# Attention's probability transposes in 64-row halves on two row tiles, and the last 64 keys' product in two 64-column tiles

## The chip, the cores and the metric

One core of a Trainium2 chip runs the program once. The metric is device time in microseconds (us) of one execution. A run's profile names the core's engines: PE is TensorE's matmul side and PEld its weight loads, DVE is VectorE, ACT is ScalarE, POOL is GpSimd, SP is SyncE.

## The reference

Attention with a learned relative-position bias, and two mixture layers behind it, all in float32:

```python
scores = scale * np.matmul(q, k.transpose(0, 1, 3, 2))
...
bias = h @ w2
scores = scores + bias.transpose(2, 0, 1)[None, :, :, :]
scores = scores - np.max(scores, axis=-1, keepdims=True)
attn = np.exp(scores)
attn = attn / (np.sum(attn, axis=-1, keepdims=True) + 1e-09)
return np.matmul(attn, v).astype(np.float32)
```

There are 4 batches, 8 heads, 576 positions and 64 values a head. The change touches the attention alone.

## The kernel before, in words

**Units, chunks and steps.** A unit is four heads of one batch (`UNITS`, 8 of them). The 576 query rows are cut into a chunk of 64 and four of 128 (`CH`); R is the rows of a chunk. A step works on one chunk, one unit and one pair of heads, so there are 80 of them. The first group of steps (`GROUPS[0]`, three units, 30 steps) also computes the bias table of each chunk as it goes; later groups have one unit each and read the finished table.

**What a step does.** `qk` (L313) makes the scores of both heads: the two heads lie on partitions 0 to 63 and 64 to 127, so their matmuls go to two row tiles (`tile_position=(64 * i, 0)`) and to separate PSUM buffers `sc`. VectorE then adds the bias and takes the row minimum of the negated scores (L328). ScalarE exponentiates and sums (L336); VectorE inverts the sums (L342, L343); GpSimd scales the rows (L345). `pv_tr` (L350) turns the probabilities, R rows of 2 x 576 keys, into nine blocks of 128 keys by R rows: eight blocks of one head each, and a ninth that holds the last 64 keys of both heads. It does three blocks per call: three transposes on TensorE into one PSUM bank (L358), and one copy into the SBUF buffer `eT`, by ScalarE (L361) or VectorE (L363) as the strings `EVAC0` and `EVAC` say. `pv` (L365) multiplies V with these blocks: the eight blocks in two column tiles, one per head (L373), and the ninth block with a 128-column matrix `vt` that has each head's last 64 keys in its own rows and columns and zeros elsewhere (L375). ScalarE copies the result out (L378), and one DMA per two steps writes it to HBM (L380).

A float32 matmul leaves two records in the trace and a transpose one, so a step has 8 records at L325, 9 at L358, 16 at L373 and 2 at L375.

**Order.** The steps are pipelined by hand. In one pass of the loop in `emit` (L382) step s has its scores, step s-1 its exponentials and sums, step s-3 its transposes and step s-4 its product with V. The strings `ORDER0` (first group) and `ORDER` (later groups) give the order in which the pass issues them: Q0 and Q1 are the two heads' scores and reductions, X0 and X1 the exponentials, T0 to T2 the three calls of `pv_tr`, P the product, N the normalisation, S other loads and preparations, B a piece of the bias. Each engine takes its instructions in that order. S also holds the conversion of the next layer's weights, on ScalarE and VectorE.

**PSUM.** The scores use four banks. The four others (`banks`, L139) rotate: each call of `mix` (L145) takes the next, whoever used it last. A later taker waits for the earlier one's copy.

Of the kernel before, what the change touches and what calls it, by code (L numbers as in the profile page):

```python
# [15 lines left out]
B, H, S, D = 4, 8, 576, 64  # L16
P = 128
# [7 lines left out]
GROUPS = [[0, 1, 2], [3], [4], [5], [6], [7]]  # L25
# [4 lines left out]

ORDER0 = "Q0 T0 X0 B Q1 X1 B S T1 B P B B B N T2"
ORDER = "T0 S T1 X0 X1 Q0 Q1 P N T2"

OUT = {"A": "AAA", "D": "AVV", "T": "VAA"}

EVAC0 = "VAAVAV"
EVAC = "VAVAAV"

# [90 lines left out]
def flat(t):  # L133
    return t.rearrange("p a b -> p (a b)")
# [24 lines left out]
class Attn(Base):  # L159
# [74 lines left out]
    def bias_mm(self, c, blk, ts):  # L234
        nc = self.nc
        r0, R = CH[c]
        ncg = 4 // (R // 64)
        kind = KIND[c][blk]
        pb = self.mix([4 * R], "pb")
        for cg in range(4):  # L240
            nc.tensor.matmul(pb[32 * cg:32 * cg + 32, :], self.w2b[:, 0, :], flat(ts[cg // ncg][:, cg % ncg]),
                             start=True, stop=True, tile_position=(0, 32 * cg))
        i = self.bti = getattr(self, "bti", -1) + 1
        bt = self.tl(f"bt{i % 2}", [4, R])
        pv = pb.rearrange("p (a r) -> p a r", a=4)
        if kind == "A":
            (nc.scalar.copy if OUT["A"][0] == "A" else nc.vector.tensor_copy)(bt, pv)
        elif kind == "D":
            if OUT["D"][0] == "A":
                nc.scalar.activation(bt, pv, AF.Identity, bias=self.cb)  # L250
            else:
                nc.vector.tensor_scalar(bt, pv, self.cb, None, op0=ALU.add)
        else:
            nc.vector.scalar_tensor_tensor(bt, self.lib[c][0][:, 0:1, :].to_broadcast([P, 4, R]), self.cb, pv, op0=ALU.mult, op1=ALU.add)
        return bt
# [94 lines left out]
    def pv_tr(self, c, u, pr, es, eT, gi):  # L350
        nc = self.nc
        r0, R = CH[c]
        e, st = es
        ef = flat(e[:R])
        src = [ef[:, j * 640 + kb * 128:j * 640 + (kb + 1) * 128] for kb in range(4) for j in range(2)] + [ef[:, 512:640]]
        pt = self.mix([3, 128], "pt")
        for i in range(3):
            nc.tensor.transpose(pt[:, i, :R], src[3 * gi + i], self.ident[:R, :R])  # L358
        d = eT[:, 3 * gi:3 * gi + 3, :]
        if (EVAC0 if u in GROUPS[0] else EVAC)[3 * pr + gi] == "A":  # L360
            nc.scalar.copy(d, pt[:, :, :R])  # L361
        else:
            nc.vector.tensor_copy(d, pt[:, :, :R])  # L363

    def pv(self, s, c, u, pr, eT):  # L365
        nc = self.nc
        b, hf = UNITS[u]
        r0, R = CH[c]
        vm, vt = self.v[u]
        po = self.mix([R], "po")  # L370
        for kb in range(4):
            for j in range(2):
                nc.tensor.matmul(po[64 * j:64 * j + 64, :], vm[:, 2 * pr + j, kb, :], eT[:, 2 * kb + j, :],  # L373
                                 start=kb == 0, stop=False, tile_position=(0, 64 * j), skip_group_check=True)
        nc.tensor.matmul(po, vt[:, pr, :], eT[:, 8, :], start=False, stop=True, skip_group_check=True)  # L375
        if pr == 0:
            self.xo = self.tl(f"xo{s // 2 % 2}", [2, R])
        nc.scalar.copy(self.xo[:, pr, :], po)  # L378
        if pr == 1:
            nc.sync.dma_start(self.xT_d[2 * hf:2 * hf + 2, :, b * S + r0:b * S + r0 + R].rearrange("q p r -> p q r"), self.xo)  # L380

    def emit(self, extra):  # L382
# [89 lines left out]
        for s in range(N + 4):  # L472
# [16 lines left out]
            if a:  # L489
                es[s] = self.new_e(s)  # L490
            for k in (ORDER0 if g0 else ORDER).split():
                if k[0] == "Q" and a:
# [888 lines left out]
```

## Time and profile before

| | |
|---|---|
| median of 3 runs | 1086.18 us (1084.26 to 1088.27) |
| the profiled execution | 1088.37 us, span 1086.6 us |
| TensorE | 1044.1 us busy, 96% of the span |
| VectorE | 617.9 us busy, 57% |
| ScalarE | 538.7 us busy, 50% |
| GpSimd | 220.7 us busy, 20% |

A row of a timeline gives start and length in us, then engine, line, operation, the tile written and the tile read, the partitions and columns, how many instructions the row merges, and in brackets how long the engine was idle before and what ended that. A row of groups gives the count, the busy time and the mean length of one. A row of stretches gives, for each engine, its busy time and its number of instructions.

### The profile page before, as it was taken

Reading aid. Unit: us, or ns where it says so; the run is one execution under the profiler, and the core shown is the slowest. Engines: PE = TensorE matmul, PEld = TensorE weight load, DVE = VectorE, ACT = ScalarE, POOL = GpSimd, SP = SyncE. Lnnn points to the kernel's source line nnn. Section 1 sums busy time; section 2 is a strip of 40 time slices with the busy share of each in tenths; the row PEclk is TensorE's granted clock in tenths of the full one; section 3 lists DMA queues with packets and bytes.
Section 4 is the critical chain, followed back from the end, with each engine's and each line's share of the span. In section 5 each row is a group of like instructions: output and inputs, shape, how many; then the busy total and the mean of one; then the engine's idle time right before and its main releaser. Section 6 shows DMA issues by size and latency. Waiting matters only on the chain. (4 is left out here: it accounts for less than half of the span.)

```text
span 1086.6 us, 20980 instructions
## 1 busy us (share of the span) xinstructions
PE 1044.1 (96%) x7637; PEld 814.8 (75%) x7637; DVE 617.9 (57%) x1554; ACT 538.7 (50%) x1198; POOL 220.7 (20%) x273
## 2 busy tenths in 40 slices
PE   5999999999999989999999999999999989999996
PEld 2355556767777778988888889888887868777774
DVE  4886875678776776776354443436364634345320
ACT  4778777667776655544343333333343223354421
POOL 0132223444444300000011000001311242221111
PEclk9999999999999999999999999999999989999998
DMA  7565582333233233431102010110412175676840
GB/s 237 178 191 167 162 274 58 94 96 96 79 83 108 70 110 104 129 117 58 59 21 40 1 40 8 33 39 2 152 64 41 48 254 213 245 289 263 335 165 34
DMA packets 62192, 129.19 MB, mean 119 GB/s; under 512 B 13820, under 2 KB 35708, under 8 KB 59264
## 3 DMA queue, kind: packets, MB, share of 16 engines
q1 hardware_dynamic: 57424, 117.69, 33.1%
q0 software_dynamic: 4512, 9.49, 3.0%
q8 instruction: 62, 1.02, 0.4%
q10 hardware_dynamic: 144, 0.59, 0.2%
q14 instruction: 50, 0.41, 0.2%
HBM read 164.08 MB, written 14.65 MB: 164 GB/s over the span
## 5 line engine op out<-in xcount | busy, mean ns | idle before, releaser
L701 PE MATMUL acc<-wp,g 128*128 128x512 f32 x864 | 225.4, 396 | 0.7 <-DVE t L678 0.6
L671 PE MATMUL ph<-xh,wp 128*128 128x256 f32 x1024 | 207.1, 285 | 1.6 <-ACT y L714 1.2
L345 POOL TENSOR_SCALAR e<-e,st 128x576 f32<-128x576 f32 (+1 forms) x160 | 126.6, 803 | 244.2 <-DVE st L343 190.2
L671 PEld LDWEIGHTS ph<-xh,wp 128*128 128x128 f32 x1024 | 166.4, 189 | 10.9 <-issue 3.9
L701 PEld LDWEIGHTS acc<-wp,g 128*128 128x128 f32 x864 | 153.1, 189 | 27.6 <-DVE t L678 1.2
L328 DVE CUSTOM_DVE_ANT_0 e<-sc,bias 128x576 f32<-128x576 f32 (+1 forms) x160 | 116.4, 751 | 62.4 <-PE sc L325 60.1
L671 PE MATMUL ph<-xl,wp 128*128 128x256 f32 x512 | 144.3, 282 | 0.3 <-DVE xl L657 0.3
L677 ACT ACTIVATE r<-ph,small 128x256 f32<-128x256 f32 x144 | 67.5, 469 | 123.4 <-PE ph L671 118.3
L336 ACT ACTIVATE e<-e,st 128x576 f32<-128x576 f32 (+1 forms) x160 | 123.0, 775 | 0.0
L678 DVE SCALAR_TENSOR_TENSOR t<-r,ph 128x256 f32<-128x256 f32 x144 | 60.3, 419 | 107.4 <-ACT r L677 99.6
L680 ACT ACTIVATE g<-t 128x256 fp32r<-128x256 f32 x144 | 60.2, 418 | 115.0 <-DVE t L678 114.1
L1024 PE MATMUL peh<-ws,xt 128*128 128x512 f32 x408 | 102.7, 405 | 4.5 <-PEq L1333 4.4
L325 PE MATMUL sc<-K,q 64*128 64x288 f32 (+1 forms) x640 | 101.9, 425 | 0.0
L358 PE MATMUL pt<-cst,e 128*128 128x128 f32 (+1 forms) x720 | 97.8, 268 | 2.7 <-ACT eT L361 1.4
L358 PEld LDWEIGHTS pt<-cst,e 128*128 128x128 f32 (+1 forms) x720 | 75.8, 141 | 31.9 <-issue 14.9
L671 PEld LDWEIGHTS ph<-xl,wp 128*128 128x128 f32 x512 | 96.7, 189 | 3.9 <-DVE xl L657 0.5
L775 POOL DMA_INDIRECT tab_d<-small x18 | 18.5, 1029 | 379.5 <-DVE small L773 343.5
L1024 PEld LDWEIGHTS peh<-ws,xt 128*128 128x128 f32 x408 | 76.9, 192 | 22.5 <-issue 5.0
L683 DVE SCALAR_TENSOR_TENSOR g<-t,g 128x256 fp32r<-128x256 f32 x144 | 61.1, 424 | 56.1 <-ACT g L680 55.7
L1052 PE MATMUL peo<-ws,ehh 128*128 128x512 f32 x272 | 86.1, 398 | 0.0
L373 PEld LDWEIGHTS po<-eT,V 128*64 128x64 f32 x1280 | 63.3, 136 | 24.6 <-issue 18.5
L373 PE MATMUL po<-eT,V 128*64 128x128 f32 (+1 forms) x1280 | 81.2, 269 | 0.0
(215 smaller groups left out, 1451.5 us busy)
## 6 DMA issues: line engine op xcount, KB each, us to landing
er<-in_we SPq DMA_DIRECT2D x46, 1024.0 KB
er<-in_we SPq DMA_DIRECT2D x86, 512.0 KB
xb<-in_xb SPq DMA_DIRECT2D x38, 512.0 KB
wraw<-in_wf SPq DMA_DIRECT2D x32, 512.0 KB
cv<-in_xb SPq DMA_DIRECT2D x11, 512.0 KB
K<-in_kT SPq DMA_DIRECT2D x8, 576.0 KB
xr<-xT_d SPq DMA_DIRECT2D x9, 512.0 KB
y_d<-y SPq DMA_DIRECT2D x18, 256.0 KB
```

Source lines behind the costliest of these rows:

```text
L325: nc.tensor.matmul(self.sc[i][:R, n, :288], q[d, pr, :], self.kv[u][d, pr, n * 288:(n + 1) * 288], start=True, stop=True, tile_position=(6 ...
L328: nc.vector.tensor_tensor_reduce(out=e[:R, j, :].rearrange("p (n s) -> p n s", n=2), in0=self.sc[j][:R, :, :288], in1=self.bias[c][:R, 4 * ...
L336: self.nc.scalar.activation(e[:R, j, :], e[:R, j, :], AF.Exp, scale=-1.0, bias=st[:R, j:j + 1], accum_out=st[:R, 4 + j:5 + j])
L345: nc.gpsimd.tensor_scalar(e[:R, j, :], e[:R, j, :], st[:R, 6 + j:7 + j], 1.0, op0=ALU.mult, op1=ALU.mult)
L358: nc.tensor.transpose(pt[:, i, :R], src[3 * gi + i], self.ident[:R, :R])
L373: nc.tensor.matmul(po[64 * j:64 * j + 64, :], vm[:, 2 * pr + j, kb, :], eT[:, 2 * kb + j, :], start=kb == 0, stop=False, tile_position=(0, ...
L671: nc.tensor.matmul(ph, w, x[c], start=n == 0, stop=n == 11)
L677: nc.scalar.activation(r, ph, AF.Relu, bias=self.three)
L683: nc.vector.scalar_tensor_tensor(g[:, 1], t, 1.0 / 6.0, g[:, 0].bitcast(F32), op0=ALU.mult, op1=ALU.subtract)
L701: nc.tensor.matmul(acc[t], x, w, start=f == 0 and i == 0, stop=f == 15 and i == 2)
L1024: nc.tensor.matmul(ph[:, n, :], a, w, start=c == 0 and i == 0, stop=c == 3 and i == 2)
L1052: nc.tensor.matmul(d["po"], a, w, start=f == 0 and i == 0, stop=f == 7 and i == 2)
```

## The change

The nine blocks of a step are transposed in two calls instead of three, the first with five blocks and the second with four. In a chunk of 128 rows each block is transposed as two halves of 64 rows, each half on a row tile of its own and into a PSUM bank of its own; ScalarE copies the lower halves out and VectorE the upper ones. In the chunk of 64 rows there is one half; ScalarE copies the first call's blocks and VectorE the second's. The ninth block's product with `vt` is issued as two matmuls of 64 columns, in the column tiles of the other eight. T2 leaves the orders.

```diff
-ORDER0 = "Q0 T0 X0 B Q1 X1 B S T1 B P B B B N T2"
-ORDER = "T0 S T1 X0 X1 Q0 Q1 P N T2"
+ORDER0 = "Q0 T0 X0 B Q1 X1 B S T1 B P B B B N"
+ORDER = "T0 S T1 X0 X1 Q0 Q1 P N"
...
-EVAC0 = "VAAVAV"
-EVAC = "VAVAAV"
+EVAC = 0
...
-        pt = self.mix([3, 128], "pt")
-        for i in range(3):
-            nc.tensor.transpose(pt[:, i, :R], src[3 * gi + i], self.ident[:R, :R])
-        d = eT[:, 3 * gi:3 * gi + 3, :]
-        if (EVAC0 if u in GROUPS[0] else EVAC)[3 * pr + gi] == "A":
-            nc.scalar.copy(d, pt[:, :, :R])
-        else:
-            nc.vector.tensor_copy(d, pt[:, :, :R])
+
+        a, z = ((0, 5), (5, 9))[gi]
+        hs = range(R // 64)
+        pts = [self.mix([z - a, 64], "pt") for _ in hs]
+        for i in range(a, z):
+            for h in hs:
+                d = slice(64 * h, 64 * h + 64)
+                nc.tensor.transpose(pts[h][:, i - a, :], src[i][d], self.ident[d, d], tile_position=(64 * h, 0))
+        for h in hs:
+            d = eT[:, a:z, 64 * h:64 * h + 64]
+            if (h if R == 128 else gi) == EVAC:
+                nc.scalar.copy(d, pts[h])
+            else:
+                nc.vector.tensor_copy(d, pts[h])
...
-        nc.tensor.matmul(po, vt[:, pr, :], eT[:, 8, :], start=False, stop=True, skip_group_check=True)
+
+        for j in range(2):
+            nc.tensor.matmul(po[64 * j:64 * j + 64, :], vt[:, pr, 64 * j:64 * j + 64], eT[:, 8, :],
+                             start=False, stop=True, tile_position=(0, 64 * j), skip_group_check=True)
```

## Rows read from the trace of the kernel before

**Rows 1.** The page: TensorE's busy time and the clock granted to it.

```profile
PE 1044.1 (96%) x7637; PEld 814.8 (75%) x7637; DVE 617.9 (57%) x1554; ACT 538.7 (50%) x1198; POOL 220.7 (20%) x273
...
PEclk9999999999999999999999999999999989999998
```

**Rows 2.** Groups at L325 on TensorE, from 85.1 to 172.7 and 195.8 to 368.7.

```profile
L325 PE MATMUL sc<-K,q 64*128 64x288 f32 x112 | 17.4, 429 | 0.0
...
L325 PE MATMUL sc<-K,q 64*128 64x288 f32 (+1 forms) x392 | 63.4, 425 | 0.0
```

**Rows 3.** Stretches: length, PE, PEld, DVE, ACT, POOL, clock, DMA share, GB/s.

```profile
85.10:172.70 87.60, 86.22 (x739) 51.58 (x738) 63.40 (x147) 69.57 (x153) 22.97 (x28) 1.00 0.60 191
...
195.80:368.70 172.90, 171.46 (x1717) 128.94 (x1715) 127.91 (x385) 121.16 (x328) 77.61 (x108) 1.00 0.34 94
```

**Rows 4.** Timeline of TensorE's matmuls over one step of 128 rows.

```profile
333.01 0.49 PE L375 MATMUL po<-eT,VT 128*128 128x128 f32 x2
333.34 1.15 PE L358 MATMUL pt<-cst,e 128*128 128x128 f32 x9
334.41 1.24 PE L325 MATMUL sc<-K,q 64*128 64x288 f32 x8
335.58 1.09 PE L373 MATMUL po<-eT,V 128*64 128x128 f32 x16
336.61 0.38 PE L375 MATMUL po<-eT,VT 128*128 128x128 f32 x1
```

**Rows 5.** Timeline of TensorE's weight loads over the same step.

```profile
333.23 1.02 PEld L358 LDWEIGHTS pt<-cst,e 128*128 128x128 f32 x9
334.41 0.79 PEld L325 LDWEIGHTS sc<-K,q 64*128 64x128 f32 x8 [0.17 <-issue]
335.58 0.85 PEld L373 LDWEIGHTS po<-eT,V 128*64 128x64 f32 x16 [0.39 <-issue]
```

**Rows 6.** Timeline of TensorE and its loads, transposes of a 64-row chunk.

```profile
316.01 0.77 PE L358 MATMUL pt<-cst,e 64*128 64x64 f32 x9
316.62 1.82 PE L325 MATMUL sc<-K,q 64*128 64x288 f32 x8
...
316.00 0.63 PEld L358 LDWEIGHTS pt<-cst,e 64*128 64x128 f32 x9
```

**Rows 7.** Timeline of the weight loads that start between 334.40 and 334.45.

```profile
334.41 0.19 PEld L325 LDWEIGHTS sc<-K,q 64*128 64x128 f32 x2 [0.17 <-issue]
```

**Rows 8.** Groups of the copies out of PSUM after transposes, by form.

```profile
L363 DVE COPY eT<-pt 128x384 f32<-128x384 f32 x96 | 51.5, 550 | 3.7 <-PE pt L358 3.6
...
L361 ACT COPY eT<-pt 128x384 f32<-128x384 f32 x96 | 44.7, 482 | 23.7 <-PE pt L358 17.6 <-DVE eT L363 2.9 <-DVE st L342 1.5
...
L363 DVE COPY eT<-pt 128x192 f32<-128x192 f32 x24 | 8.3, 344 | 0.0
L361 ACT COPY eT<-pt 128x192 f32<-128x192 f32 x24 | 7.2, 317 | 3.9 <-DVE eT L363 1.9 <-PE pt L358 1.8 <-ACT xo L378 0.2
```

**Rows 9.** Timeline of VectorE, the reductions of the step of rows 4.

```profile
335.79 0.76 DVE L328 CUSTOM_DVE_ANT_0 e<-sc,bias 128x576 f32<-128x576 f32 x1 [0.91 <-PE sc L325]
...
336.48 0.75 DVE L328 CUSTOM_DVE_ANT_0 e<-sc,bias 128x576 f32<-128x576 f32 x1
```

**Rows 10.** Timeline of ScalarE in that step: output copy and an exponential.

```profile
333.54 0.27 ACT L378 COPY xo<-po 128x128 f32<-128x128 f32 x1 [0.52 <-PE po L375]
...
334.94 0.78 ACT L336 ACTIVATE e<-e,st 128x576 f32<-128x576 f32 x1
```

**Rows 11.** Timeline of TensorE, two score starts of the first group without bias work.

```profile
172.76 1.24 PE L325 MATMUL sc<-K,q 64*128 64x288 f32 x8
...
176.51 0.76 PE L325 MATMUL sc<-K,q 64*128 64x288 f32 x4
```

**Rows 12.** Timeline of TensorE, three transposes in a bias step, then the product.

```profile
112.39 0.49 PE L358 MATMUL pt<-cst,e 128*128 128x128 f32 x3
112.81 1.09 PE L373 MATMUL po<-eT,V 128*64 128x128 f32 x16
```

## The prediction, made before any run of the changed kernel

> **What bounds the kernel now.** I read the page first, then the busy time by stage, then one step of the attention on TensorE, and only then the waits. The page says that TensorE is busy 96% of the span at full granted clock [rows 1]. That alone proves little, because the ends of matmuls are modelled, so I look for the stage that the change touches. Score matmuls leave eight records a step, and by their count [rows 2] the stretch from 85.1 to 172.7 us, which also builds the bias, has 112 / 8 = 14 steps of 6.26 us, and the stretch from 195.8 to 368.7 has 49 steps of 3.53 us. In the second, TensorE is busy for 171.46 us of 172.90, VectorE for 127.91 (74%), ScalarE for 121.16 (70%) [rows 3]. What the reader should see in one step of it [rows 4] is that every start on TensorE follows from the one before: V tail 333.01, transposes 333.34, scores 334.41, PV 335.58, next V tail 336.61. The terms are 0.33 + 1.07 + 1.17 + 1.03 = 3.60 us, which is the whole step. So time taken off TensorE here is time taken off the span, until another engine's loop is as long.
>
> **Transposes.** Nine 128-row transposes cost 1.07 us up to the first score matmul [rows 4]; nine of 64 rows, in the steps of the first query chunk, cost 0.61 us (316.01 to 316.62) [rows 6]. Their nine weight loads fill 0.63 us, the last alone 0.14, so one follows the other every (0.63 - 0.14) / 8 = 0.061 us. The change makes two such half transposes of each 128-row one, on two row tiles. The question is whether the two halves of a pair run beside each other. No transpose in this trace does so. The nearest row is the scores, also 64-row operands on two row tiles with outputs in banks of their own: two of their loads, each 0.18 us long or more, cover 0.19 us together [rows 7], so they lie beside each other. I take the same for the transposes: 0.61 us in place of 1.07. The other end is one after the other, 0.61 + 9 x 0.061 = 1.16 us, a loss of 0.09.
>
> The Trainium skill, TensorE: Matmul & The Clock Gate, section LDWEIGHTS, says that a load takes its columns divided by 1.2 GHz, however many rows it has. By that a half load of 128 columns would last 0.107 us, an estimate from that page; nine pairs side by side would take 0.96 us and the transposes would gain next to nothing. The 0.061 us of [rows 6] speaks against it for transposes, and the measurement decides.
>
> **V tail.** The tail (two records over 128 columns) becomes four records in the two 64-column tiles that PV already uses. PV's 16 loads fill 0.85 us, the last 0.14 or so [rows 5]: eight pairs, (0.85 - 0.14) / 7 = 0.10 us each. Two pairs more make PV 1.03 + 0.21 = 1.24 us, and the 0.33 us of the old tail go. Two changes of tile shape go with them: between PV and the old tail (inside the 0.33), and between transposes and scores, where 0.17 us of "issue" now stand before the scores' loads [rows 5] (inside 1.07 - 0.61, since the 64-row steps don't pay it).
>
> **Sum for TensorE, per step:** 0.61 + 1.17 + 1.24 = 3.02 us against 3.60, a gain of 0.58. With halves one by one: 1.16 + 1.17 + 1.24 = 3.57, a gain of 0.03.
>
> **Copies.** Three copies of 128x384 a step, shared evenly between ScalarE (0.482 us) and VectorE (0.550), become four, one of 320 and one of 256 columns on each. From the 384 and 192 forms [rows 8], a column costs 0.86 ns on ScalarE and 1.07 on VectorE, so each engine's pair costs 0.80 and 0.90 us instead of 0.72 and 0.83 (1.5 copies): some 0.08 us a step more on each, hidden beside TensorE while those engines have slack. ScalarE does 121.16 / 49 = 2.47 us a step and VectorE 2.61 [rows 3], so 2.55 and 2.69 under a step of 3.02. That is 84 to 89%, no longer roomy. For it, the halves of a group are copied by two engines at once, which shortens the wait for a transposed block.
>
> **What is late next.** Score buffers: scores start at 334.41 [rows 4], the first reduction at 335.79, the second at 336.48, and it lasts 0.75 [rows 9]; so the next scores can't start before 337.23, a loop of 2.82 us, just under 3.02. PSUM banks: a step takes two, two and one of the four rotating banks instead of one four times, so the upper half of the second group waits for the previous step's output copy. Now that copy starts at 333.54 and takes 0.27 us, after ScalarE had been idle for 0.52 [rows 10]; it ends 0.58 us after the next transposes' first load at 333.23 [rows 5]. The new half comes some 0.17 us (tile change) and 5 x 0.061 us later than that load: about 0.1 us of stall, behind which scores and PV stand in TensorE's queue. Conversion work for the next layer also lands on both engines in part of these steps. For all three I take 0.13 us: a step of 3.15 us.
>
> **Stages.** The 49 steps: 3.53 - 3.15 = 0.38 each, 18.6 us. The six steps between the two stretches pay 3.75 now (172.76 to 176.51) [rows 11] and have the same work after: 0.60 each, 3.6 us. Bias steps: three runs of three transposes, each like the 0.42 us from 112.39 to 112.81 [rows 12], become 9 x 0.061 = 0.55, a gain of 0.71; 0.17 goes between scores and first transposes, 0.12 with the tail, and two to three changes of tile shape come up where 128-row bias transposes stood next to transposes or tail (0.34 to 0.51). That is 0.5 to 0.65. ScalarE is busy for 79% there (69.57 of 87.6) [rows 3] and copies stand behind its long bias instructions, so I count 0.30 for 18 bias steps with 128 rows (14 in [rows 2] and four before): 5.4 us. Nothing for the first steps, whose inputs are still being loaded. No DMA is moved past another: SP and POOL issue what they did in the order they did. Moving the last group of transposes ahead of PV costs nothing by itself: PV reads blocks transposed a step earlier. The layers behind keep TensorE busy too [rows 1], so I let the gain through whole.
>
> Total: 18.6 + 3.6 + 5.4 = 27.6 us. The profiled execution took 1088.37 us (span 1086.6), 2.2 above the median; 1088.4 - 27.6 = 1060.8, or 1059 against the median of 1086.2. A difference of 0.5%, 5.4 us, is about what a measurement of this kernel can tell from none.
>
> **Rivals.**
> 1. *Copies and reductions become the bound.* For it: the loop of 2.82 us and 89% of VectorE. Against: VectorE now waits 0.91 us for TensorE before the reductions [rows 9]. If VectorE's copies slip into the loop by half, a step takes about 3.35: gain 0.18 x 49 = 8.8 us, the six steps 0.40 each, the bias steps nothing: 11 in all, 1075 us. The Trainium skill, TensorEngine Tiling (Array Packing), Performance Considerations, warns that after a tiling speed-up the PSUM copy may become the bound; by that rule this case holds. The 74 and 70% of [rows 3] neither prove nor exclude it.
> 2. *The pairs don't overlap*, and the change doesn't do what it looks like. Gain 0.03 x 49 = 1.5 us, lost again where the bias steps change shape: 1086 us. Against it only [rows 7], on another kind of matmul.
> 3. *Slower: the fifth bank.* If the output copy comes behind one more exponential (0.78 us) [rows 10] and then takes 0.27, each step stalls about 1.0 us; the point from which it decides is 0.58. Then (1.0 - 0.58) x 49 = 21 us slower: 1107. Against it: ScalarE's idle 0.52 before that copy.
> 4. *A half load costs what a whole one does.* 128-row loads follow each other every (1.02 - 0.14) / 8 = 0.11 us [rows 5]; 18 of them one by one take 1.98 us, a step 1.98 + 0.05 + 1.17 + 1.24 = 4.44, 0.84 worse: 41 us, 1127. Speaks against it: [rows 6].
>
> **How the numbers follow.** Forecast (gain 15 to 44): 0.66. Rival 1 (gain 6 to 15): 0.14. Rival 2: 0.10. Rivals 3 and 4: 0.07 and 0.03. Faster 0.80, same 0.10, slower 0.10. The range goes from the full sum, 0.58 x 49 + 0.72 x 6 + 0.55 x 18 = 43 us (1043, and a microsecond for the last steps: 1042), to just beyond rival 1 (1080); 0.8 of the chance lies inside.
>
> **What would show it.** Right: the two halves of a transpose starting within 0.01 us of each other, pairs every 0.06; no "issue" idle between transposes and scores; steps of 3.0 to 3.2 us over the last 49; VectorE and ScalarE nearer 85% there. Wrong: pairs at 0.12 us or more; TensorE waiting for the output copy or the reductions in every step; ScalarE or VectorE without idle time.

## The result, and the profile after

The changed kernel takes 1075.0 us (median of 4 runs, 1073.36 to 1078.48) against 1087.22 beside it: a ratio of 0.9896, 95% interval 0.9863 to 0.9929. It is faster by about 1%, some 12 us, where the prediction had 27.6. A second measurement beside the last experiments gave 0.9893 (0.9864 to 0.9922). The two profiled executions stand 1088.37 - 1073.36 = 15.0 us apart, so the traces account for 15.

The page of the changed kernel: busy time of each engine, then the granted clock in 40 slices of the span.

```profile
PE 1014.0 (95%) x8373; PEld 799.7 (75%) x8373; DVE 620.8 (58%) x1578; ACT 539.5 (50%) x1222; POOL 220.6 (21%) x273
...
PEclk9999999989999989999999999999999989999998
```

TensorE has 30 us less to do than in [rows 1] and the span is only 15 us shorter. The clock row has two dips (slices 9 and 15) that the kernel before does not have there; slice 15 (from 375 us) lies behind the attention, and a second profile of the changed kernel shows no dip in it.

The stretches of the changed kernel that hold the same 14 and the same 49 steps as those of [rows 3]:

```profile
84.65:170.34 85.69, 78.09 (x897) 48.62 (x893) 64.00 (x154) 69.71 (x159) 22.71 (x28) 1.00 0.59 194
191.63:353.95 162.32, 154.72 (x2167) 120.31 (x2165) 128.98 (x400) 122.26 (x342) 77.08 (x107) 0.98 0.36 101
```

TensorE's busy time fell from 86.22 to 78.09 us and from 171.46 to 154.72, but its idle time rose from 1.4 to 7.6 us in both: it now waits.

One undisturbed step on TensorE, the counterpart of [rows 4] (start, length, engine, line, operation):

```profile
319.76 0.39 PE L382 MATMUL po<-eT,VT 128*64 128x128 f32 x4
320.08 0.90 PE L362 MATMUL pt<-cst,e 64*128 64x64 f32 x18
320.76 1.25 PE L324 MATMUL sc<-K,q 64*128 64x288 f32 x8
321.93 1.09 PE L378 MATMUL po<-eT,V 128*64 128x128 f32 x16
322.86 0.39 PE L382 MATMUL po<-eT,VT 128*64 128x128 f32 x4
323.18 0.34 PE L362 MATMUL pt<-cst,e 64*128 64x64 f32 x4
```

From 320.08 to 323.18 the step takes 3.10 us: transposes 0.68, scores 1.17, PV and tail 1.25. The kernel before needed 3.60.

The weight loads of the transposes, first those that start between 323.17 and 323.45, the five pairs of the first call, then those between 323.17 and 323.20 alone:

```profile
323.18 0.39 PEld L362 LDWEIGHTS pt<-cst,e 64*128 64x128 f32 x10 [0.17 <-issue]
...
323.18 0.14 PEld L362 LDWEIGHTS pt<-cst,e 64*128 64x128 f32 x2 [0.17 <-issue]
```

Two loads of 0.13 to 0.14 us each cover 0.14 together: the halves of a pair lie beside each other. Ten fill 0.39, so the five pairs follow each other every (0.39 - 0.14) / 4 = 0.062 us. In the second call the upper halves wait 0.07 us for their bank.

So the mechanism is there and the clean step is right. To see where the rest went, take the first score matmul of each step (step 0 is the first) and subtract, in us:

```
steps                    before   after
0 to 30, first group     167.94   164.07
30 to 37                  23.58    20.67
37 to 40                  12.82    16.14
40 to 70                 105.72    98.66
70 to 79                  30.77    26.86
after 79, other layers   717.83   717.64
```

In the stretch 70 to 79 the gain is 3.91 / 9 = 0.43 us a step; over 49 steps that would be 21. Between steps 37 and 70, where the next layer's weights are converted, 11 of them are missing. The first group gave 3.9 in place of 9.0 in this pair of profiles. The layers behind gave nothing back.

Steps 37 to 40 hold the largest single loss. ScalarE there:

```profile
212.23 0.43 ACT L366 COPY eT<-pt 128x320 f32<-128x320 f32 x1 [0.23 <-PE pt L362]
216.90 0.66 ACT L611 ACTIVATE cva<-wraw 128x512 f32<-128x512 f32 x1 [4.24 <-DMA wraw<-in_wf]
217.46 0.36 ACT L366 COPY eT<-pt 128x256 f32<-128x256 f32 x1
...
219.24 0.25 ACT L386 COPY xo<-po 128x128 f32<-128x128 f32 x1
```

And TensorE:

```profile
214.72 0.27 PE L362 MATMUL pt<-cst,e 64*128 64x64 f32 x1
217.87 0.79 PE L362 MATMUL pt<-cst,e 64*128 64x64 f32 x10 [2.88 <-ACT eT L366]
219.54 0.68 PE L362 MATMUL pt<-cst,e 64*128 64x64 f32 x7 [0.88 <-ACT xo L386]
219.92 2.33 PE L324 MATMUL sc<-K,q 64*128 64x288 f32 x8
222.18 1.97 PE L378 MATMUL po<-eT,V 128*64 128x128 f32 x16
```

ScalarE stands for 4.24 us in front of a cast whose weights have not landed; behind it in its queue are the copies that free PSUM banks (at 217.46 the first of them). TensorE stops at the second transpose of the first pair, then again for the output copy's bank, and then runs scores in 2.33 us and PV in 1.97, about twice the lengths above.

### The profile page after: what moved, and what is told of

Read it like the earlier page. It is cut to its first block, busy times and chain, and to the rows that moved or that the text cites. A ratio compares the mean times of both kernels' runs of the same rounds, so it can differ in the third digit from the quotient of the medians.

```text
span 1071.6 us, 22490 instructions
## 1 busy us (share of the span) xinstructions
PE 1014.0 (95%) x8373; PEld 799.7 (75%) x8373; DVE 620.8 (58%) x1578; ACT 539.5 (50%) x1222; POOL 220.6 (21%) x273
## 5 line engine op out<-in xcount | busy, mean ns | idle before, releaser
L324 PE MATMUL sc<-K,q 64*128 64x288 f32 (+1 forms) x640 | 104.6, 426 | 0.4 <-DVE st L327 0.4
L362 PEld LDWEIGHTS pt<-cst,e 64*128 64x128 f32 x1296 | 60.3, 139 | 34.5 <-issue 10.4
L362 PE MATMUL pt<-cst,e 64*128 64x64 f32 x1296 | 72.6, 232 | 8.6 <-ACT eT L366 3.5
```

The lines of the kernel that those rows point to most:

```text
L324: nc.tensor.matmul(self.sc[i][:R, n, :288], q[d, pr, :], self.kv[u][d, pr, n * 288:(n + 1) * 288], start=True, stop=True, tile_position=(6 ...
L362: nc.tensor.transpose(pts[h][:, i - a, :], src[i][d], self.ident[d, d], tile_position=(64 * h, 0))
```

## The experiments

Every kernel was timed beside the kernel before on the same chip:

```
kernel             median us   ratio to before   interval
after_late         1067.71     0.9860            0.9837 to 0.9883
before_late        1079.20     0.9960            0.9944 to 0.9975
only_transposes    1082.85     0.9982            0.9970 to 0.9993
only_tail          1082.29     0.9977            0.9961 to 0.9992
late_spread        1062.38     0.9798            0.9778 to 0.9819
late_pool          1065.69     0.9825            0.9804 to 0.9846
late_xo_v          1067.13     0.9852            0.9831 to 0.9874
late_g0old         1063.91     0.9817            0.9794 to 0.9840
g0old_spread       1060.99     0.9780            0.9752 to 0.9808
g0old_spread_pool  1060.82     0.9777            0.9747 to 0.9806
g0four             1073.92     0.9895            0.9864 to 0.9926
after_again        1072.99     0.9893            0.9864 to 0.9922
```

Stretches of steps, where given, are of each kernel's one profile. The stretch of the first group scatters from profile to profile of kernels that are equal there (162.8 to 168.8 us for the five with the new transposes and nothing else changed there), so for that stage the ratios count. Differences of ratios are given in points, hundredths of the time of the kernel before.

**The two parts of the change.** `only_transposes` undoes the tail:

```diff
-        for j in range(2):
-            nc.tensor.matmul(po[64 * j:64 * j + 64, :], vt[:, pr, 64 * j:64 * j + 64], eT[:, 8, :],
-                             start=False, stop=True, tile_position=(0, 64 * j), skip_group_check=True)
+        nc.tensor.matmul(po, vt[:, pr, :], eT[:, 8, :], start=False, stop=True, skip_group_check=True)
```

> The changed kernel with the last 64 keys' product again as one matmul of 128 columns. By the working of the prediction the tail's part is 0.33 - 0.21 = 0.12 us a step, so 0.12 x 79 = 9 us at most, and no less than the clean steps show: theory W expects 4 to 8 us slower than the changed kernel; a rival, that the tail's split brings nothing since the tile shape changes before the next transposes anyway, expects within 2 us.

`only_tail` is the kernel before with the same lines exchanged the other way.

> The kernel before with only the last 64 keys' product in two 64-column tiles. The tail saves one change of tile shape before itself but needs one after itself, since the transposes there still have 128 rows: 0.33 us go, 0.21 and 0.17 come, so within 3 us of the kernel before. The rival, that the tail is worth 0.12 us a step by itself, expects 6 to 9 us faster.

Measured: 0.9982 and 0.9977, and 0.9896 with both. The parts do not add. TensorE in clean steps of `only_transposes`:

```profile
359.10 1.24 PE L324 MATMUL sc<-K,q 64*128 64x288 f32 x8
360.27 1.09 PE L378 MATMUL po<-eT,V 128*64 128x128 f32 x16
361.30 0.49 PE L381 MATMUL po<-eT,VT 128*128 128x128 f32 x2
361.71 0.88 PE L362 MATMUL pt<-cst,e 64*128 64x64 f32 x18
362.38 0.52 PE L324 MATMUL sc<-K,q 64*128 64x288 f32 x2
```

And of `only_tail`:

```profile
357.96 1.24 PE L325 MATMUL sc<-K,q 64*128 64x288 f32 x8
359.13 1.09 PE L373 MATMUL po<-eT,V 128*64 128x128 f32 x16
360.06 0.39 PE L376 MATMUL po<-eT,VT 128*64 128x128 f32 x4
360.38 1.20 PE L358 MATMUL pt<-cst,e 128*128 128x128 f32 x9
361.51 0.51 PE L325 MATMUL sc<-K,q 64*128 64x288 f32 x2
```

The steps take 3.28 and 3.55 us against 3.60 before and 3.10 with both. The split tail alone is worth 0.05 in such a step, nearly nothing, and 2.5 us in all, within the 3 expected: PV and tail take 1.25 us up to the transposes (359.13 to 360.38) where [rows 4] had 1.03 + 0.33, but the transposes then take 1.13 instead of 1.07. With the halves a change of tile shape in front of the transposes is there anyway; then PV and an undivided tail take 1.44 us (360.27 to 361.71) and the split one 1.25, so it is worth 0.19. `only_transposes` is 0.86 points slower than the changed kernel, 9 us, somewhat more than the 4 to 8 expected.

**The weight conversion: the wait.** Two kernels begin the cast, the first instruction of each early conversion, one pass later, `after_late` from the changed kernel and `before_late` from the one before:

```diff
-        return [load, first, lambda: S["f"][1](), lambda: S["f"][2](), lambda: S["f"][3](nc.vector)]
+        return [load, lambda: None, first, lambda: S["f"][1](), lambda: S["f"][2](), lambda: S["f"][3](nc.vector)]
```

> The changed kernel, with each of the four early weight conversions begun one pass later after its load (the conversion's first cast stands two passes behind the load and not one). Theory W: the 10 us that the changed kernel loses in the passes with conversions come mostly from ScalarE standing in its queue behind a cast whose weights have not landed (4.24 us once, 7.1 us in all), so TensorE runs out of free banks; without that wait the time falls by 5 to 9 us against the changed kernel. Rival S: ScalarE and VectorE are simply too busy in those passes, whatever the order; then the time falls by less than 2 us.

> The kernel before with the same delay of the casts. Theory W: the kernel before loses only about 1.6 us of TensorE to that wait, so it gains 1 to 2.5 us. Rival S: no difference that can be measured (within 1 us).

Steps 37 to 40 fall from 16.14 to 10.74 us in the changed kernel, and from 12.82 to 10.79 in the one before, so the wait is the cause there and costs the changed kernel 5.4 us, the one before 2.0. By the ratio `after_late` gains 0.33 to 0.36 points, some 4 us, less than the 5 to 9 expected and more than rival S allows; the two intervals overlap, so it is the trace that shows this wait gone, not the ratio. `before_late` gains 4.3 us, more than expected: besides the 2.0, 2.2 more went in steps 40 to 70. So both kernels pay for that wait about as much by the ratio, and the rest of the changed kernel's loss lies elsewhere. What is left shows it: in steps 40 to 70 `before_late` takes 103.55 us, and three times the last ten, clean steps of the kernel before (334.41 to 368.78, 34.37 us) are 103.1; `after_late` takes 97.46 where three times those of the changed kernel (323.86 to 353.95, 30.09 us) are 90.3. The shorter step has no room for the conversion, the longer one had.

**The weight conversion: VectorE.** VectorE in `after_late`, one conversion pass:

```profile
278.27 0.47 DVE L368 COPY eT<-pt 128x320 f32<-128x320 f32 x1
278.66 1.17 DVE L617 SCALAR_TENSOR_TENSOR cvb<-wraw,cvb 128x512 int32<-128x512 int32 x1
279.86 1.12 DVE L618 SCALAR_TENSOR_TENSOR cvb<-cva,cvb 128x512 int32<-128x512 int32 x1
280.90 0.41 DVE L368 COPY eT<-pt 128x256 f32<-128x256 f32 x1
281.24 0.74 DVE L327 CUSTOM_DVE_ANT_0 e<-sc,bias 128x576 f32<-128x576 f32 x1
...
281.91 0.75 DVE L327 CUSTOM_DVE_ANT_0 e<-sc,bias 128x576 f32<-128x576 f32 x1
```

GpSimd beside it, and the next scores on TensorE:

```profile
278.55 1.90 POOL L344 TENSOR_SCALAR e<-e,st 128x576 f32<-128x576 f32 x2 [1.54 <-DVE st L342]
...
282.04 1.91 PE L324 MATMUL sc<-K,q 64*128 64x288 f32 x8 [0.21 <-DVE st L327]
```

No row of VectorE has idle time in front of it: two conversion instructions push the reductions back, and the next scores wait for these. Part of the peak may be GpSimd's: in this profile the same two instructions last 0.68 and 0.69 us on the mean where no scaling runs beside them, here 1.17 and 1.12, and the two scalings take 1.90 us where a clean step has 1.47. No run separates this. `late_spread` gives each of the two a pass of its own:

```diff
-        return [load, lambda: None, first, lambda: S["f"][1](), lambda: S["f"][2](), lambda: S["f"][3](nc.vector)]
+        return [load, lambda: None, first, lambda: S["f"][1](), lambda: S["f"][4](), lambda: S["f"][5](), lambda: S["f"][3](nc.vector)]
```

where entries 4 and 5 are the two halves of entry 2.

> after_late with the third piece of each early conversion, two VectorE instructions of together 2.29 us, spread over two passes. Theory V: with the late cast, what the changed kernel still loses in the passes with conversions (97.46 us for 30 steps where the clean ones take 3 x 30.1 = 90.3) is VectorE's peak, more than a pass can hold beside 2.7 us of attention work, so spreading it takes 1.5 to 4 us off. Rival: the sum of work counts, not its peak, or ScalarE and the banks do; then within 1 us of after_late.

`late_pool` puts the last subtraction on GpSimd:

```diff
-        return [load, lambda: None, first, lambda: S["f"][1](), lambda: S["f"][2](), lambda: S["f"][3](nc.vector)]
+        return [load, lambda: None, first, lambda: S["f"][1](), lambda: S["f"][2](), lambda: S["f"][3](nc.gpsimd)]
```

> after_late with the last subtraction of each early conversion (1.0 to 1.15 us on VectorE) on GpSimd. Theory V: VectorE has 4 us less to do in the passes with conversions, so 1 to 3 us faster than after_late. Rival: GpSimd's scaling of the probabilities comes late behind it and the transposes wait for that, so 1 to 4 us slower.

Steps 40 to 70 take 94.66 us in `late_spread` and 95.70 in `late_pool` instead of 97.46, gains of 2.8 and 1.8, both inside theory V's. The ratios are 0.62 and 0.35 points better, 6.7 and 3.8 us; what exceeds the stretch is not accounted for, the first group of `late_spread`'s profile was even longer. VectorE's peak is the second part of the loss. A clean rate would give 90.3, so 4 us of these steps stay open.

**The first group.** TensorE's waits there, from 60 to 190 us, in the changed kernel (line, what it waited for, us in all, times, longest):

```profile
PE pbt L263 <- ACT bt L246: 2.8, 2, 2.7
PE po L378 <- ACT eT L366: 2.4, 8, 0.3
PE pbt L263 <- ACT eT L366: 1.4, 1, 1.4
PE pbt L263 <- DVE bt L253: 1.2, 1, 1.2
PE po L378 <- DVE eT L368: 1.1, 1, 1.1
PE pb L240 <- ACT bias L277: 0.9, 3, 0.4
```

They sum to 12.1 us with the smaller rows. The same view of the kernel before sums to 5.4:

```profile
PE pb L241 <- ACT bt L247: 2.7, 2, 2.5
PE pb L241 <- DVE bt L254: 1.9, 2, 1.6
PE pt L358 <- ACT bt L250: 0.8, 1, 0.8
```

All but 0.3 us (for a bias input) are waits for a copy, in front of every kind of PSUM taker. Two experiments ask which resource it is. `late_xo_v` relieves ScalarE:

```diff
-        nc.scalar.copy(self.xo[:, pr, :], po)
+        (nc.vector.tensor_copy if u in GROUPS[0] else nc.scalar.copy)(self.xo[:, pr, :], po)
```

> after_late with the output copy of the first group's units on VectorE in place of ScalarE. Theory A: in the bias steps TensorE now waits for copies that stand in ScalarE's queue (81% busy there, VectorE 75%), so taking 0.27 us a step from it shortens the 30 steps of the first group by 2 to 5 us. Rival: the bias steps go by the loads of the bias inputs or by both engines together; then within 2 us either way.

0.9852 against 0.9860, and TensorE's waits sum to 12.0 us: ScalarE's queue alone is not it. `late_g0old` goes back to the old transposes in the first group:

```diff
+        if self.g0:
+            pt = self.mix([3, 128], "pt")
+            for i in range(3):
+                nc.tensor.transpose(pt[:, i, :R], src[3 * gi + i], self.ident[:R, :R])
...
+            return
```

with the old `ORDER0` and the old choice of engines.

> after_late with the old transposes (three calls, 128 rows, three banks) in the first group only; the V tail stays split. Theory B: the bias steps are no longer set by TensorE, so that giving its 0.3 to 0.5 us a step back costs only what the six steps without bias lose, 6 x 0.35 = 2.1 us, and perhaps a little; 1 to 4 us slower than after_late. Rival, the prediction's own sum: 18 x 0.3 + 6 x 0.5 = 8 us slower.

It is not slower but faster than `after_late`: 0.9817 against 0.9860, 0.43 points or 4.7 us, with the six steps without bias slower by 23.19 - 21.30 = 1.9 us as expected. So in the bias steps the halves bring nothing, and by the ratio they cost time. How much is uncertain: 3.1 of the 3.5 us between the two profiles lie behind step 79, where the kernels are equal, and the same exchange with the spread conversion (`late_spread` to `g0old_spread`, below) is worth 0.18 points, 2.0 us. From step 6 to step 24, the bias steps with 128 rows, the six profiles with old transposes take 108.8 to 113.3 us and the seven with halves 108.8 to 114.3. `g0four` has neither halves nor row tiles there, but the two calls and their four banks:

```diff
-            pt = self.mix([3, 128], "pt")
...
+            a, m, z = ((0, 3, 5), (5, 7, 9))[gi]
+            parts = ((a, m), (m, z))
+            pts = [self.mix([q - p, 128], "pt") for p, q in parts]
```

> late_g0old with its 128-row transposes in two calls and four banks in the first group (two copies a call, as the changed kernel has), no row tiles. Theory F: in the bias steps it is the number of banks that a step takes, and with it the copies that TensorE waits for, which costs time; so TensorE's waits from 60 to 190 us rise from 4.3 us towards the 12 to 13 us of the kernels with halves, and the kernel is 3 to 8 us slower than late_g0old. Rival: it is the change of tile shapes or the speed of the halves; then TensorE's waits stay at 3 to 6 us and the time within 2 us of late_g0old.

0.9895 against 0.9817, 8.5 us slower and just beyond the 3 to 8 expected, and TensorE's waits sum to 11.1 us, all for copies, against 4.3 in `late_g0old`, 1.1 of them for a bias input.

The stretch from 60 to 165 us (length, busy time of PE, PEld, DVE, ACT, POOL, clock, DMA share, GB/s) in the kernel before:

```profile
60.00:165.00 105.00, 99.61 (x883) 59.26 (x884) 78.78 (x180) 80.19 (x177) 26.94 (x33) 1.00 0.63 199
```

The same stretch in the changed kernel:

```profile
60.00:165.00 105.00, 94.49 (x1057) 57.04 (x1055) 79.45 (x186) 82.73 (x189) 26.88 (x33) 0.98 0.61 200
```

In `late_g0old`:

```profile
60.00:165.00 105.00, 100.86 (x940) 59.09 (x939) 81.13 (x181) 83.30 (x188) 29.23 (x34) 1.00 0.64 203
```

In `g0four`:

```profile
60.00:165.00 105.00, 95.39 (x890) 55.81 (x887) 78.42 (x183) 79.42 (x181) 26.32 (x31) 0.99 0.57 182
```

TensorE is idle for 10 us in the two kernels that take five banks a step and for 4 to 5 in the two that take four, whether the transposes are halves or whole. This is what theory F expects: the banks that a step takes, and the copies that must free them, cost the time. `g0four` also issues its transposes in two calls and makes four copies in place of three, so the number of banks, that of copies and the order of taking them are not separated. Nor does it give the changed kernel's own loss: in the steps of 64 rows it takes five banks where the changed kernel takes three, and 5.8 us of what it loses in its profile lie before step 6 (37.94 us against 32.16).

**Together.** `g0old_spread` has old transposes in the first group, halves after it, the late cast and the spread conversion; `g0old_spread_pool` the subtraction on GpSimd too. Both are the edits above, joined.

> late_g0old with the spread conversion of late_spread. If the two losses are separate (the first group's copies, the conversion passes), their gains over after_late add: late_spread was 0.6 points of the ratio better, late_g0old 0.4, so a ratio of 0.974 to 0.978, some 25 us faster than the kernel before. Rival: both gains were chance of the loads in the first group; then 0.980 or above.

> The same with the last subtraction of each early conversion on GpSimd too. If VectorE still sets the conversion passes after the spread (94.66 us for 30 steps where clean ones take 90.3), 1 to 2 us faster than g0old_spread; rival: with the peak gone GpSimd's delay of the scaling counts, and it is the same or 1 us slower.

0.9780 and 0.9777, some 24 us faster than the kernel before, 12 faster than the changed kernel, and about 20 by the ratio faster than `before_late`, which has the late cast without the change. The kernel before with the spread conversion was not run; its conversion passes have little left to gain (103.55 us where clean ones take 103.1). The ratios stand at the upper edge of what the sum of both gains allowed. GpSimd's part is 1.65 us in steps 40 to 70 (94.90 to 93.25) and nothing that the ratio can tell; the last 3 us to the clean 90.3 stay open.

**The changed kernel again.**

> The changed kernel once more, beside the others on the same chip: a ratio of 0.986 to 0.993 as measured before. A second profile shows which of its waits repeat: every theory expects the ScalarE wait for the first converted weights (4 us) and TensorE waits of 10 us or more in the first group again.

The ratio is 0.9893, the wait for the first weights 3.9 us, TensorE's waits in the first group 11.6 us: all repeat.

## Why the prediction was right and where it was wrong

The mechanism on TensorE was right. The gain was some 12 us (15 in the two profiles) in place of 27.6, because two terms of the sum failed: the 18.6 us of the 49 steps and the 9.0 of the first group.

- *Transposes.* Right: the halves run beside each other, as the scores in [rows 7] do, and pairs follow every 0.062 us, as the 64-row transposes of [rows 6] do. The run is 0.68 us instead of 0.61 because the second call waits 0.07 for the output copy's bank, which the prediction had at about 0.1. Rivals 2 and 4 are out. The Trainium skill (TensorE: Matmul & The Clock Gate, section LDWEIGHTS) would give each load 0.107 us, an estimate from its rule; the trace does not agree with that for transposes.
- *V tail and sum for TensorE.* Right: 1.25 us against 1.24, and 3.10 against 3.02. Not said in it: most of the tail's worth depends on the halves.
- *Copies.* Right: 0.425 and 0.373 us on ScalarE, 0.483 and 0.416 on VectorE are 0.80 and 0.90 us a step, the two numbers of the prediction.
- *"For all three I take 0.13 us: a step of 3.15 us."* This failed. The bank wait in it is 0.07 us, and a clean step of 128 rows takes 3.10, better than 3.15. But the 49 steps take 162.33 / 49 = 3.31 on the average, where ten clean ones, two of them with 64 rows, take 30.09 / 10 = 3.01: the conversions cost 0.30 a step, against 3.53 - 3.44 = 0.09 in the kernel before. The prediction named the conversion work and then spread it as an average over all steps, without adding its instructions to a single pass. A pass with 2.3 us of conversion on VectorE beside 2.4 of attention can't be 3.1 long. In ten clean steps VectorE is busy for 23.53 us of 34.37 before and for 23.73 of 30.09 after, so it had 1.1 us a step free and now has 0.64; the 2.61 and 2.69 of the prediction, and the 2.7 expected of `late_spread`, have the conversions in them. The kernel before took the conversion in over a few passes; the changed one can't. The term of 18.6 us measured 10.6; the clean rate would have given 21. That 18.6 is not farther off is in part luck: it takes 3.15, a step of 128 rows, from 3.53, a mean that has the shorter steps of 64 rows in it.
- *"I count 0.30 for 18 bias steps", and 0.60 for the six without bias.* This failed too. In the 14 bias steps of [rows 3] TensorE's work did fall, by 8.1 us or 0.58 a step, inside the 0.5 to 0.65 of the prediction; its idle time grew by 6.2, so the steps gained 2.0 us, 0.14 each. Over all 18 it is 3.0 us in place of 5.4 in this pair of profiles, and over all profiles no gain is to be seen. The prediction looked at one bank wait, the output copy's in clean steps, and not at the first group, where bias blocks take from the same four banks. `late_g0old` and `g0four` show that there the extra banks cost about what the halves save, or more. Of the six steps, five gained 0.41 each, since the product now waits 0.3 us for the copy of the first call's lower halves to free its bank, and the last lost 0.18: 1.8 us in place of 3.6.
- *Rival 1* gave the measured time, 1075 us, with a step of 3.35 on the average, against 3.31. That is luck in part: it had VectorE's copies slip into every step, but the clean steps go by TensorE's own work but for 0.07 us, and VectorE sets the pace in conversion passes alone. The rule of the Trainium skill beside it (TensorEngine Tiling (Array Packing), Performance Considerations: after a tiling speed-up the PSUM copy may become the bound) agrees with the first group, where TensorE's waits rose from 5.4 to 12.1 us, nearly all of them for copies.
- *Rival 3* named the right resource, the fifth bank. In clean steps it costs 0.07 us and not 1.0; it costs more where a bias copy or a late cast stands in front of the copy.

## What to carry to other kernels

Before a time saved on one engine is multiplied by the number of steps, put every instruction of the fullest step, not of the mean one, against the new length of a step. Count how many buffers of a rotation a step takes before and after; a change that takes more of them couples the engines more tightly just where it makes the step shorter. Two changes of tile shape in one loop have to be priced together, since removing one alone may only move it.

## What the runs showed of the hardware that was not expected

The granted clock fell to its lower level after TensorE had waited 2.88 us for a bank. The changed kernel's stretches after that wait (columns as in [rows 3]):

```profile
217.80:222.20 4.40, 3.45 (x27) 2.41 (x27) 1.88 (x5) 3.91 (x12) 1.63 (x2) 0.51 0.21 51
222.20:225.20 3.00, 3.00 (x39) 2.67 (x40) 1.70 (x7) 0.27 (x1) 0.98 (x2) 0.58 0.04 13
225.20:228.00 2.80, 2.80 (x46) 2.21 (x42) 2.77 (x7) 2.48 (x7) 0.48 (x1) 1.00 0.00 0
```

The column before the last two is the granted share: 0.51 is the 1.2 GHz level of the two, and the stretch from 225.2 on is the first at 1.00 again. Scores took 2.33 us instead of 1.25 and PV 1.97 instead of 1.09 meanwhile, so (2.33 - 1.25) + (1.97 - 1.09) = 2.0 us of that step's loss are the clock's and not the wait's. In the kernel before, the same cast held TensorE for 1.37 us, and the clock of that slice did not dip. The wait of 2.7 us in the changed kernel's first group (to 81.75) has a clock of 0.50 behind it too, from 81.7 to 84; the one of 2.5 us in the kernel before (to 83.64) does not, with 1.00 from 83.6 to 85.
